# One decode block on one core: the third load of wo moved ahead of two loads of values, and 128 rows of w2 loaded by GpSimd to 32 partitions

## The chip, the core and the metric

The kernel runs on one NeuronCore of a Trainium2 chip. The core has five engines with instruction streams of their own: TensorE (PE, with its weight loads as PEld), VectorE (DVE), ScalarE (ACT), GpSimd (POOL) and SyncE (SP), and sixteen DMA engines that move data between HBM and the on-chip memory (SBUF, 128 partitions). The metric is the device time of one execution in microseconds (us); lower is better.

## What is computed

One token goes through an attention block and a second block, and the results are added. Cut to what matters:

```python
xn = layernorm(x)                                   # x: 1024 values
# A: 32 query heads, 4 key/value heads, 65536 positions of 128
q = xn @ wq                                         # wq 1024 x 4096
p = softmax(q . k_cache / sqrt(128));  o = p . v_cache
A = o @ wo                                          # wo 4096 x 1024
# B
h  = gelu(layernorm(xn) @ w1)                       # w1 1024 x 1024
hs = shift(h) @ w2                                  # shifts along a sequence of length 1
x1 = xn + hs                                        # w2 1024 x 1024
B  = x1 + gelu(layernorm(x1) @ w3) @ w4             # w3 1024 x 3584, w4 3584 x 1024
out = x + A + B
```

All inputs are bf16. With a sequence of one token every shift pushes its value out, so the vector that meets w2 is zero; the kernel loads w2 all the same and multiplies it by a zero vector (`g_bf`). The weights and the two caches together are 162 MiB, and each byte is read once.

## The kernel before, in words

**Slots and loads.** SBUF holds eight slots of 16 KB per partition (`slots_sb`). A load of a 4 MB piece of keys or values fills two slots (32 KB to each of the 128 partitions); a load of wo, w1 or w2 fills one (2 MB, 16 KB to each partition). All these loads are issued by SP, in one fixed order, on one DMA queue (q1 in the profile): `load` (line 315), `load2` (line 321) and, for the last pieces of w4, `load_pieces` (line 328). Before each issue SP waits (line 54) until the last user of the slot is done. So one load that waits for its slot holds back every load behind it in SP's order, even one whose own slot has long been free.

**The order.** `loads` (line 625) begins with wq in two loads, w1, w2 and w3 in two. Then `order` (line 632) alternates keys and values, values lagging five tiles behind, and ends by hand with the last values and the four loads of wo; w4 follows in three groups (line 639), the last one in pieces of two, one and one row per partition. `where` (line 301) gives each load its slots: values alternate between slots 4-5 and 0-1, so value tile 14 waits for the use of tile 12, and tile 15 for that of tile 13; wo 0 to 3 go to slots 2, 3, 6 and 7, the last two of which held the last keys; w4 goes to 4-5, 0 and 1.

**A head.** DVE turns each half tile of keys by a transpose (line 542) into the buffer `X`, PE forms the scores (line 555), ACT takes the exponentials (line 580), PE and ACT transpose them (lines 589, 592), and PE adds up the values (line 603). `combine` (line 610) gives the head's output, which `use_wo` (line 531) multiplies with its part of wo. The buffer `X` has two halves: half 0 is first used by the first transpose of keys, half 1 also by the small products.

**The small products.** `rows_mv` (line 454) issues the matmuls of a weight: for each row index of a partition and each quarter of the columns one matmul of 256 columns (line 460), so 32 for a weight of 1024 x 1024. A weight of 1024 rows stands as eight rows of 2 KB in each of 128 partitions. `use_w2` (line 509) adds the product to `xn`, normalizes the sum, and gives `xn3_bf` for w3.

**The beginning.** POOL sets constants until 8.15 us (lines 386 to 408) and has nothing to do later but one small power in each of three layer norms (line 446). ACT issues three small loads of x (lines 411 and 417) on a queue of its own (q10). DVE waits for them (line 420), and the first layer norm follows.

**The end.** PE multiplies the pieces of w4 as they land, DVE adds the result to the rest (`fin`, line 716), and SP and ACT issue the store (line 719).

Of the kernel before, what the change touches and what calls it, by code (L numbers as in the profile page):

```python
# [6 lines left out]
BF = mybir.dt.bfloat16  # L7
# [82 lines left out]
def _deps(q, reads, writes):  # L90
    for b in reads:
        for s, v in b.w.items():
            q.wait((s, v))
    for b in writes:
        for s, v in b.w.items():
            q.wait((s, v))
        for s, v in b.r.items():
            q.wait((s, v))


def _done(ev, reads, writes, partial=False):
    for b in reads:
        b.add_read(ev)
    for b in writes:
        if partial:
            b.add_write(ev)
        else:
            b.set_write(ev)


def _op(q, fn, reads=(), writes=(), partial=False):
    _deps(q, reads, writes)
    ev = q.op(fn, True)
    _done(ev, reads, writes, partial)
    return ev


def _grp(q, fns, reads=(), writes=(), partial=False):
    _deps(q, reads, writes)
    ev = None  # L120
    for i, fn in enumerate(fns):
        ev = q.op(fn, i == len(fns) - 1)
    _done(ev, reads, writes, partial)
    return ev
# [23 lines left out]
def _dma(q, chan, fn, reads=(), writes=(), partial=False):  # L148
    _deps(q, reads, writes)
    chan.n += 1  # L150
    ev = q.dma(fn, chan.sem, 16 * chan.n)
    _done(ev, reads, writes, partial)
    return ev
# [10 lines left out]
def bass_parallel_sum__gqa_block_cached__mixer_s_mlp__decode_kernel(  # L164
# [14 lines left out]
    P = 128  # L179
    D = A_x.shape[2]  # L180
# [5 lines left out]
    R = D // P  # L186
# [10 lines left out]
    EPS = 1e-5  # L197
    NS = 8
    PAD = 31
    SLOT = 8192  # L200

    with ExitStack() as es:
# [3 lines left out]
        def sb(name, shape, dt):  # L206
            return E(nc.sbuf_tensor(name, shape, dt))

        def ps(name, shape, dt):
            return E(nc.psum_tensor(name, shape, dt))  # L210

        def sem(name):
            return E(nc.semaphore(name))
# [25 lines left out]
        Ycur = sb("Ycur", [P, 4, 4, G], BF)  # L239
        slots_sb = sb("slots_sb", [P, NS, SLOT], BF)  # L240
        X = sb("X", [P, 2, SLOT], BF)
        S_sb = sb("S_sb", [P, NCH, 512], F32)
# [11 lines left out]
        cb_o = sb("cb_o", [P, R], F32)  # L254
        oP_bf = sb("oP_bf", [P, HKV, PAD + R + PAD], BF)
        xr_bf = sb("xr_bf", [P, RW], BF)
        accr = sb("accr", [P, RW], F32)
        g_bf = sb("g_bf", [P, R + 32], BF)
# [3 lines left out]
        h1g_bf = sb("h1g_bf", [P, R], BF)  # L262
        gh_bf = sb("gh_bf", [P, PAD + NT + PAD], BF)
        fin = sb("fin", [P, RW], BF)

        S_all = ps("S_ps", [P, 4 * 512], F32)
        S_ps = [S_all[:, 512 * i:512 * (i + 1)] for i in range(4)]
# [6 lines left out]
        q_dve = _Q("dve", sem("c_dve"))  # L274
        q_act = _Q("act", sem("c_act"))
        q_pool = _Q("pool", sem("c_pool"))
        q_sp = _Q("sp", None)
        ch_x = _DmaChan(sem("d_x"))
        ch_out = _DmaChan(sem("d_out"))
        ch_v = [_DmaChan(sem("d_v0")), _DmaChan(sem("d_v1"))]  # L280
        t_x, t_s, t_r, t_p, t_t, t_o = [sem("t_" + c) for c in "xsrpto"]
# [3 lines left out]
        b_const = _B(); b_xb = _B(); b_x = _B(); b_xn = _B(); b_xn2 = _B(); b_x1 = _B(); b_xn3 = _B()  # L285
        b_ln = _B(); b_qT = _B(); b_Y = _B(); b_Yc = _B(); b_misc = _B(); b_ge = _B()
        b_X = [_B(), _B()]
# [10 lines left out]
        X32 = X[:].bitcast(F32)  # L298
# [11 lines left out]
        def take(i, n, uses):  # L310
            for k in range(n):
                assert taken[i + k] == 0
                taken[i + k] = uses

        def load(i, src, width=SLOT):
            take(i, 1, 1)
            view = slots_sb[:, i, 0:width]
            _dma(q_sp, slots[i].chan, lambda e, view=view, src=src: e.dma_start(out=view, in_=src), writes=[slots[i].buf])
            return [(view, [slots[i].buf], i)]

        def load2(i, src, half=SLOT, chan=None):
            take(i, 2, 1 if half == SLOT else 2)
            view = slots_sb[:, i:i + 2, :].rearrange("p s c -> p (s c)")[:, 0:2 * half]
            _dma(q_sp, chan or slots[i].chan, lambda e, view=view, src=src: e.dma_start(out=view, in_=src), writes=[slots[i].buf, slots[i + 1].buf])
            bufs = [[slots[i].buf], [slots[i + 1].buf]] if half == SLOT else [[slots[i].buf, slots[i + 1].buf]] * 2
            return [(view[:, k * half:(k + 1) * half], bufs[k], i + k) for k in range(2)]
# [16 lines left out]

        wq_v = A_wq.rearrange("(p r) n -> p (r n)", p=P)
        w1_v = B_w1.rearrange("(p r) n -> p (r n)", p=P)
        w2_v = B_w2.rearrange("(p r) n -> p (r n)", p=P)
        w3_v = B_w3.rearrange("(p r) n -> p (r n)", p=P)
        w4_v = B_w4.rearrange("(p r) n -> p (r n)", p=P)

# [30 lines left out]
            return load2(i, A_v_cache[0, h, a * n:(a + 1) * n, :].rearrange("(p c) d -> p (c d)", p=P), chan=ch_v[a % 2])  # L380


        evs = []
        for t_, val in ((selGT_bf, 1.0), (selTT, 1.0), (ident_bf, 0.0), (ones_f, 1.0), (neghalf, -0.5), (permWE, 1.0), (maskA, 1.0),
                        (sel16, 1.0), (dmask, 0.0), (g_bf, 0.0), (xn_bf, 0.0), (xn2_bf, 0.0), (xn3_bf, 0.0), (oP_bf, 0.0), (gh_bf, 0.0)):
# [22 lines left out]
                                                          compare_op=ALU.not_equal, fill=1.0, base=-16 * j, channel_multiplier=1))  # L408
        b_const.set_write(ev)

        _dma(q_act, ch_x, lambda e: e.dma_start(out=xP_bf[:, :], in_=A_x[0, 0, :].rearrange("(p r) -> p r", p=P)), writes=[b_xb])
        _op(q_dve, lambda e: e.memset(xr_bf[:], 0.0), writes=[b_xr])
        x4 = A_x[0, 0, :].rearrange("(j m) -> j m", j=4)
        _deps(q_act, [], [b_xr])
        for j in (0, 2):
            ch_x.n += 1
            q_act.dma(lambda e, j=j: e.dma_start(out=xr_bf[32 * j + PAD:32 * j + PAD + 2, :], in_=x4[j:j + 2, :]), ch_x.sem, 16 * ch_x.n)
        b_xr.set_write((ch_x.sem, 16 * ch_x.n))
# [35 lines left out]
        def rows_mv(nkk, parts, st_fn, b_st, b_slot, b_out, first, last, k0=0):  # L454
            fns = []
            for kk in range(k0, k0 + nkk):
                for out_fn, mv_fn in parts:
                    for j in range(4):
                        fns.append(lambda e, kk=kk, j=j, out_fn=out_fn, mv_fn=mv_fn, st=(first and kk == k0), sp=(last and kk == k0 + nkk - 1):
                                   e.matmul(out_fn(j), st_fn(kk, j), mv_fn(kk, j), start=st, stop=sp, tile_position=(0, 32 * j), skip_group_check=True))  # L460
            _grp(q_pe, fns, reads=b_slot + [b_st], writes=b_out, partial=not first)

        def to_p(src, c0, n, b_src):
            _op(q_dve, lambda e: e.transpose(out=X32[:, 1, c0:c0 + 32 * n], in_=src), reads=b_src, writes=[b_X[1]], partial=c0 > 0)  # L464
# [31 lines left out]
        def at_border(vec, kk, t):  # L496
            c = kk + PAD * (t % 2)
            return vec[:, c:c + 32]

        def d_parts(view, c0):  # L500
            return [(lambda t: M1_ps[32 * t:32 * t + 32, c0:c0 + RW], lambda kk, t: view[:, kk * D + t * RW:kk * D + (t + 1) * RW])]
# [6 lines left out]

        def use_w2(ld):
            view, b = ld[0:2]  # L510
            rows_mv(R, d_parts(view, 0), lambda kk, t: g_bf[:, kk:kk + 32], b_const, b, [b_M1], True, False)
            to_p(M1_ps[:, 0:RW].rearrange("p (c r) -> p r c", r=R), 0, R, [b_M1])
            _op(q_dve, lambda e: e.tensor_tensor(out=x1[:], in0=xn[:], in1=X32[:, 1, 0:32 * R:32], op=ALU.add), reads=[b_xn, b_X[1]], writes=[b_x1])
            layer_norm(x1, b_x1, None, xn3_bf, b_xn3, 4)

        def use_w3(j, ld):
# [4 lines left out]
            if j == 3:  # L521
                to_p(S_all[:, 1024:1024 + FW].rearrange("p (c s) -> p s c", s=NT), 0, NT, [b_S[2], b_S[3]])
                gelu(NT, gh_bf[:, PAD:PAD + NT], b_gh)

# [85 lines left out]
        def combine(h):  # L610
# [10 lines left out]
            _op(q_dve, lambda e: e.reduce_sum(cb_o[:, :], cb_m[:, :, :].rearrange("p x r -> p r x"), axis=AX.X), reads=[b_cb], writes=[b_cb])  # L621
            _op(q_act, lambda e: e.activation(oP_bf[:, h, PAD:PAD + R], cb_o[:, :], ACTF.Copy), reads=[b_cb, b_const], writes=[b_oP[h]])  # L622

# [4 lines left out]
        n_kv = 4 * HKV  # L628
        order = [("k", i) for i in range(LAG)]
        for i in range(LAG, n_kv):  # L630
            order += [("v", i - LAG), ("k", i)]
        order += [("v", n_kv - 5), ("v", n_kv - 4), ("wo", 0), ("v", n_kv - 3), ("wo", 1), ("v", n_kv - 2), ("v", n_kv - 1), ("wo", 2), ("wo", 3)]
        for kind, i in order:
            loads.append((kind,) + divmod(i, 4) if kind != "wo" else (kind, i))
            if kind != "wo":
# [7 lines left out]
        _op(q_dve, lambda e: e.tensor_scalar(out=accr[:], in0=xr_bf[:], scalar1=ln_s[:, 1:2], scalar2=ln_s[:, 4:5], op0=ALU.add, op1=ALU.mult),  # L643
            reads=[b_xr, b_ln], writes=[b_accr])
        _op(q_dve, lambda e: e.tensor_tensor(out=accr[:], in0=accr[:], in1=xr_bf[:], op=ALU.add), reads=[b_xr, b_accr], writes=[b_accr])
        loaders = {"wq": load_wq, "w1": lambda i: load(i, w1_v[:, 0:SLOT]), "w2": lambda i: load(i, w2_v), "w3": load_w3, "wo": load_wo, "w4": load_w4,
                   "k": load_k, "v": load_v}
        doubles = {"wq", "w3", "k", "v"}

# [35 lines left out]
        for it in uses:  # L685
# [16 lines left out]
            elif kind == "v":  # L702
                h, n = args
# [51 lines left out]
```

## Time and profile before

| | |
|---|---|
| median of 3 runs | 406.3 us (406.21 to 406.33) |
| the profiled execution: its time, its span | 405.76 us, 404.0 us |
| bytes read from HBM | 169.87 MB, 420 GB/s over the span |
| busy share of the span: DMA queue q1 on 16 engines | 98.3% |
| PE, PEld, DVE, ACT, POOL | 38%, 17%, 45%, 19%, 2% |
| last landing of w4, then matmul, addition, store | 401.5 us, the rest to 404.0 us |

The span runs from the first to the last instruction of the profiled execution; 1.76 us of the execution's own time lie outside it. The profile cuts the span into slices and gives for each the busy share of the engines and of the DMA engines; it lists groups of instructions with their mean duration and the idle time before them; it follows the chain of work that ended last back from the last instruction; and it can print the instructions of a stretch in order of time, or the busy time of several stretches side by side. The trace also holds a record of each DMA packet: when it began, how long it took, its bytes and its queue. It does not say which of the sixteen engines carried it.

### The profile page before, as it was taken

The numbers are of one execution on the slowest core, as the hardware profiler recorded it, in microseconds if no ns is written. First come the engines' busy times: TensorE is split into PE (matmuls) and PEld (weight loads), VectorE is DVE, ScalarE is ACT, GpSimd is POOL, SyncE is SP. The second block draws the span as 40 slices with busy tenths as digits, with TensorE's granted clock in tenths as the row PEclk, the third lists the DMA queues.
The fourth block names the chain that finished last, engine by engine and source line by source line (L and its number), as shares of the span: only waits on it lengthen the run. The fifth ranks groups of instructions, "written<-read, shape, count | busy, mean of one in ns | idle before, by whom it ended". The sixth has DMA issues, their size and how long they took to land. (4 is left out here: it accounts for less than half of the span.)

```text
span 404.0 us, 3803 instructions
## 1 busy us (share of the span) xinstructions
PE 154.8 (38%) x1615; PEld 67.8 (17%) x1615; DVE 183.8 (45%) x137; ACT 75.3 (19%) x71; POOL 7.8 (2%) x38
## 2 busy tenths in 40 slices
PE   0165323244257041344561513257215152603705
PEld 0023110011023010111320101123101012301403
DVE  0135019998747263746545364748180931000200
ACT  1000000111762010191310002813010157200000
POOL 6010000000000000000000000000000000000000
PEclk9995565555556756565575565555956555666777
DMA  8999999999999999999999999999999999899995
GB/s 357 422 415 420 458 419 420 455 417 419 443 435 415 441 441 415 435 448 415 422 454 422 419 454 425 419 444 431 419 438 441 415 425 454 334 415 436 441 414 219
DMA packets 6937, 170.00 MB, mean 421 GB/s; under 512 B 904, under 2 KB 912, under 8 KB 1296
## 3 DMA queue, kind: packets, MB, share of 16 engines
q1 hardware_dynamic: 6772, 169.87, 98.3%
q8 instruction: 6, 0.10, 0.1%
q10 hardware_dynamic: 156, 0.01, 0.0%
q14 instruction: 3, 0.02, 0.0%
HBM read 169.87 MB, written 0.00 MB: 420 GB/s over the span
## 5 line engine op out<-in xcount | busy, mean ns | idle before, releaser
L542 DVE STREAM_TRANSPOSE X<-slots_sb 128x4096 f32<-128x4096 f32 x32 | 141.2, 4428 | 84.3 <-DMA slots_sb<-in_A_k_cache_dram 84.3
L555 PE MATMUL S_ps<-X,Ycur 128*32 128x512 bf16 x512 | 57.8, 596 | 139.9 <-PEq L64 126.3
L603 PE MATMUL OT_ps<-slots_sb,pT_sb 128*32 128x512 bf16 x512 | 50.9, 568 | 22.9 <-PEq L64 22.6
L567 ACT ACTIVATE S_sb<-S_ps 128x1024 f32<-128x1024 f32 x16 | 16.4, 1026 | 181.4 <-DVE mcol L566 161.4
L555 PEld LDWEIGHTS S_ps<-X,Ycur 128*32 128x32 bf16 x512 | 16.8, 124 | 176.6 <-issue 160.9
L580 ACT ACTIVATE p_sb<-S_sb,brun 128x1024 bf16<-128x1024 f32 x16 | 40.5, 2580 | 2.5 <-DVE brun L578 2.2
L603 PEld LDWEIGHTS OT_ps<-slots_sb,pT_sb 128*32 128x32 bf16 x512 | 19.9, 132 | 48.6 <-issue 46.0
L611 DVE TENSOR_TENSOR O_m<-OT_ps,selT_f 128x512 f32<-128x512 f32 x4 | 2.8, 691 | 52.1 <-PE OT_ps L603 52.1
L589 PE MATMUL PT_ps<-ident_bf,p_sb 128*128 128x128 bf16 x128 | 16.2, 307 | 18.5 <-PEq L64 18.5
L566 DVE TENSOR_REDUCE mcol<-S_ps 128x1 f32<-128x1024 f32 x16 | 19.1, 1195 | 8.6 <-PE S_ps L555 8.6
L592 ACT ACTIVATE pT_sb<-PT_ps 128x1024 bf16<-128x1024 bf16 x16 | 16.4, 1024 | 34.3 <-PE PT_ps L589 34.3
L589 PEld LDWEIGHTS PT_ps<-ident_bf,p_sb 128*128 128x128 bf16 x128 | 12.4, 138 | 24.2 <-issue 24.2
L460 PE MATMUL S_ps<-slots_sb,xn_bf 128*32 128x512 bf16 (+1 forms) x128 | 12.3, 556 | 10.4 <-DMA slots_sb<-in_B_w_dram 9.0
L460 PE MATMUL M_ps<-slots_sb,gh_bf 128*32 128x256 bf16 x112 | 5.7, 357 | 12.0 <-DMA slots_sb<-in_B_w_dram 12.0
L471 ACT ACTIVATE ge_a<-ge_b 128x8 f32<-128x8 f32 (+1 forms) x2 | 0.4, 217 | 52.2 <-DVE ge_b L470 52.2
L716 DVE TENSOR_TENSOR fin<-accr,M_ps 128x256 bf16<-128x256 f32 x1 | 0.4, 421 | 21.2 <-PE M_ps L460 21.2
L464 DVE STREAM_TRANSPOSE X<-S_ps 128x512 f32<-128x512 f32 (+1 forms) x3 | 2.6, 850 | 14.1 <-PE S_ps L460 14.1
L420 DVE CAST xP<-xP_bf 128x8 f32<-128x8 bf16 x1 | 0.2, 172 | 16.7 <-DMA xr_bf<-in_A_x_dram 16.7
L460 PEld LDWEIGHTS S_ps<-slots_sb,xn_bf 128*32 128x32 bf16 x128 | 4.5, 134 | 16.6 <-DMA slots_sb<-in_B_w_dram 9.8
L622 ACT ACTIVATE oP_bf<-cb_o 128x8 bf16<-128x8 f32 x4 | 0.8, 210 | 33.1 <-DVE cb_o L621 33.1
L460 PEld LDWEIGHTS M_ps<-slots_sb,gh_bf 128*32 128x32 bf16 x112 | 3.5, 123 | 14.2 <-DMA slots_sb<-in_B_w_dram 13.5
L434 PE MATMUL M_ps<-ln_s,ones_f 128*128 128x1 f32 x6 | 1.5, 328 | 10.6 <-DVE ln_s L433 10.6
(88 smaller groups left out, 59.1 us busy)
## 6 DMA issues: line engine op xcount, KB each, us to landing
slots_sb<-in_A_k_cache_dram SPq DMA_DIRECT2D x16, 4096.0 KB, 27.0
slots_sb<-in_A_v_cache_dram SPq DMA_DIRECT2D x16, 4096.0 KB, 26.8
slots_sb<-in_A_wq_dram SPq DMA_DIRECT2D x2, 4096.0 KB, 16.9
slots_sb<-in_A_wo_dram SPq DMA_DIRECT2D x4, 2048.0 KB, 26.4
slots_sb<-in_B_w_dram SPq DMA_DIRECT2D x2, 3584.0 KB, 32.5
slots_sb<-in_B_w_dram SPq DMA_DIRECT2D x3, 2048.0 KB, 25.9
slots_sb<-in_B_w_dram SPq DMA_DIRECT2D x1, 4096.0 KB, 26.2
slots_sb<-in_B_w_dram SPq DMA_DIRECT2D x1, 512.0 KB, 23.0
```

Source lines behind the costliest of these rows:

```text
L434: _op(q_pe, lambda e: e.matmul(M0_ps[:, c0:c0 + 1], ones_f[:, :], ln_s[:, 0:1], start=True, stop=True), reads=[b_ln, b_const], writes=[b_M0])
L460: e.matmul(out_fn(j), st_fn(kk, j), mv_fn(kk, j), start=st, stop=sp, tile_position=(0, 32 * j), skip_group_check=True))
L464: _op(q_dve, lambda e: e.transpose(out=X32[:, 1, c0:c0 + 32 * n], in_=src), reads=b_src, writes=[b_X[1]], partial=c0 > 0)
L542: turn = lambda e: e.transpose(out=X32[:, m, :], in_=K32)
L555: fns.append(lambda e, we=we, c_mid=c_mid, mv=mv: e.matmul(S_ps[bank][32 * c_mid:32 * c_mid + 32, :], Ycur[:, we, :, :].rearrange("p a g - ...
L566: _op(q_dve, lambda e: e.reduce_max(mcol[:, x:x + 1], S2, axis=AX.X), reads=[b_S[2 * i], b_S[2 * i + 1]], writes=[b_mcol], partial=x > 0)
L567: _tell(q_act, lambda e: e.activation(S_sb[:, 2 * x:2 * x + 2, :].rearrange("p s c -> p (s c)"), S2, ACTF.Copy), t_s, reads=[b_S[2 * i], b ...
L580: fn = lambda e, x=x: e.activation(p_sb[:, :, :, :, x], S_sb[:, 2 * x:2 * x + 2, :].rearrange("p s (c i) -> p s c i", i=32), ACTF.Exp, bia ...
L589: _taking(q_pe, [(t_t, 1) if c8 else (t_p, 1)], [lambda e, i=i, c=8 * c8 + i: e.transpose(out=PT_ps[:, i * P:(i + 1) * P], in_=p_sb[:, c / ...
L592: _tell(q_act, lambda e, c8=c8: e.activation(pT_sb[:, :, 32 * c8:32 * c8 + 32, :].rearrange("p a x g -> p x a g"), PT_ps[:, :].rearrange(" ...
L603: fns.append(lambda e, cl=cl, q4=q4, x0=x0: e.matmul(OT_ps[32 * q4:32 * q4 + 32, :], pT_sb[:, a, x0:x0 + 4, :].rearrange("p x g -> p (x g) ...
L611: _op(q_dve, lambda e: e.tensor_tensor(out=O_m[:, :, :], in0=OT_ps[:, :].rearrange("p (t d) -> p t d", t=4), in1=selT_f[:, :].unsqueeze(2) ...
```

## The change

It has two parts. In SP's order the third load of wo moves from behind the last two loads of values to ahead of them. And w2 is cut: SP loads its first 896 rows as seven rows to each of the 128 partitions; the last 128 rows are loaded by POOL, in three DMAs, to 32 partitions of `X`, half 0: six rows to each of the partitions 92 to 99 (two engines), two rows to each of 4 to 19 (four engines), six rows to each of 60 to 67 (two engines). Three tiny DMAs of x, into a tensor that nobody reads, stand between them. DVE first sets six rows' width of `X`, half 0, to zero in all partitions, and `use_w2` multiplies those six rows as well, 24 matmuls; with seven rows from the slot that is 52 matmuls instead of 32. POOL's DMAs stand in its queue behind the constants and ahead of the layer norms.

```diff
+    W2B = 7
...
+        pad_sb = sb("pad_sb", [16, 6, 8], BF)
...
+        ch_w2 = _DmaChan(sem("d_w2"))
...
-        w2_v = B_w2.rearrange("(p r) n -> p (r n)", p=P)
+        w2_v = B_w2[0:W2B * P, :].rearrange("(p r) n -> p (r n)", p=P)
...
+        def load_w2_part(p0, k, n, row):
+            src = B_w2[row:row + 4 * k * n, :].rearrange("(b a r) n -> a b (r n)", a=k, b=4)
+            dst = X[p0:p0 + 4 * k, 0, 0:n * D]
+            ch_w2.n += 1
+            q_pool.dma(lambda e: e.dma_start(out=dst, in_=src), ch_w2.sem, 16 * ch_w2.n)
+            return row + 4 * k * n
+
+        def load_pad(k, at):
+            src = A_x[0, 0, 0:16 * k].rearrange("(a b c) -> a b c", a=k, b=2)[:, :, 0:4]
+            dst = pad_sb[0:k, at:at + 2, 0:4]
+            ch_w2.n += 1
+            q_pool.dma(lambda e: e.dma_start(out=dst, in_=src), ch_w2.sem, 16 * ch_w2.n)
+
+        def load_w2_parts():
+            _deps(q_pool, [], [b_X[0]])
+            load_pad(15, 0)
+            row = load_w2_part(92, 2, 6, W2B * P)
+            row = load_w2_part(4, 4, 2, row)
+            load_pad(2, 2)
+            row = load_w2_part(60, 2, 6, row)
+            load_pad(7, 4)
+            assert row == D
+            b_X[0].add_write((ch_w2.sem, 16 * ch_w2.n))
...
+        _op(q_dve, lambda e: e.memset(X32[:, 0, 0:3 * D], 0.0), writes=[b_X[0]])
+        load_w2_parts()
         _dma(q_act, ch_x, lambda e: e.dma_start(out=xP_bf[:, :], in_=A_x[0, 0, :].rearrange("(p r) -> p r", p=P)), writes=[b_xb])
         _op(q_dve, lambda e: e.memset(xr_bf[:], 0.0), writes=[b_xr])
...
-            rows_mv(R, d_parts(view, 0), lambda kk, t: g_bf[:, kk:kk + 32], b_const, b, [b_M1], True, False)
+            rows_mv(W2B, d_parts(view, 0), lambda kk, t: g_bf[:, kk:kk + 32], b_const, b, [b_M1], True, False)
+            rows_mv(6, d_parts(X[:, 0, :], 0), lambda kk, t: g_bf[:, kk:kk + 32], b_const, [b_X[0]], [b_M1], False, False)
...
-        order += [("v", n_kv - 5), ("v", n_kv - 4), ("wo", 0), ("v", n_kv - 3), ("wo", 1), ("v", n_kv - 2), ("v", n_kv - 1), ("wo", 2), ("wo", 3)]
+        order += [("v", n_kv - 5), ("v", n_kv - 4), ("wo", 0), ("v", n_kv - 3), ("wo", 1), ("wo", 2), ("v", n_kv - 2), ("v", n_kv - 1), ("wo", 3)]
...
-        loaders = {"wq": load_wq, "w1": lambda i: load(i, w1_v[:, 0:SLOT]), "w2": lambda i: load(i, w2_v), "w3": load_w3, "wo": load_wo, "w4": load_w4,
+        loaders = {"wq": load_wq, "w1": lambda i: load(i, w1_v[:, 0:SLOT]), "w2": lambda i: load(i, w2_v, W2B * D), "w3": load_w3, "wo": load_wo, "w4": load_w4,
```

## The prediction, as it went on record

> **What bounds the kernel now.** I read the page's table of DMA queues first, then the chain of work that ended last, then the busy time of stretches around the one weak slice of the DMA row, and the instructions there in order of time.
>
> ```profile
> q1 hardware_dynamic: 6772, 169.87, 98.3%
> ...
> DMA 6%; PE 1%; SPq 0%; DVE 0%; issue 0%
> ```
>
> The one queue of big loads keeps the sixteen DMA engines 98.3% busy, while the busiest compute engine, DVE, stands at 45%. The chain in order of time (start, duration, what) shows the end:
>
> ```profile
> 377.57 0.43 SPq L339
> 378.00 0.04 issue
> 378.05 23.44 DMA slots_sb<-in_B_w_dram
> 401.49 0.04 issue
> 401.53 0.32 PE M_ps L460 x4
> 401.85 0.02 issue
> 401.88 0.42 DVE fin L716
> ```
>
> The last pieces of w4 are issued 23 us before they land: at the end the stream of loads is the limit, and whatever brings its last landing forward brings the end forward, one for one. Where does the stream lose time? Stretches (start:end, length, busy PE, PEld, DVE, ACT, POOL with counts, clock, DMA share, GB/s):
>
> ```profile
> 340.00:350.00 10.00, 5.19 (x48) 3.27 (x52) 0.00 (x0) 3.97 (x4) 0.00 (x0) 0.50 0.96 413
> 350.00:354.00 4.00, 2.81 (x48) 1.19 (x40) 0.00 (x0) 0.00 (x0) 0.00 (x0) 0.93 0.61 197
> 354.00:364.00 10.00, 0.27 (x4) 0.17 (x8) 0.00 (x0) 0.00 (x0) 0.00 (x0) 0.67 1.06 459
> ...
> 399.00:400.00 1.00, 1.00 (x32) 0.74 (x32) 0.00 (x0) 0.00 (x0) 0.00 (x0) 1.00 0.42 150
> 400.00:401.00 1.00, 0.55 (x16) 0.23 (x12) 0.00 (x0) 0.00 (x0) 0.00 (x0) 1.00 0.13 43
> ```
>
> There are two losses: a hole at 350 to 354, and a last stretch in which few engines still move. The hole is SP's wait:
>
> ```profile
> 332.42 0.43 SPq L318 DMA_DIRECT2D slots_sb<-in_A_wo_dram  x1
> ...
> 347.81 0.17 PEld L603 LDWEIGHTS OT_ps<-slots_sb,pT_sb 128*32 128x32 bf16 x8 [1.59 <-issue]
> ...
> 351.18 2.08 SPq L324 DMA_DIRECT2D slots_sb<-in_A_v_cache_dram  x2
> 353.30 0.94 SPq L318 DMA_DIRECT2D slots_sb<-in_A_wo_dram  x2
> ```
>
> After wo's second load (332.42) SP issues nothing until PE, which begins on value tile 12 at 347.8, has freed its slots (351.18). Meanwhile the queue runs dry. The two loads of wo behind the wait need no such slot.
>
> **The hole, engine by engine.** I strung the packet records into sixteen chains: a packet begins within some 5 ns of the end of the one before on its engine. A 32 KB packet takes 1.213 us on every chain, a 16 KB one 0.61. At the hole ten chains fall idle between 350.1 and 350.75, two at 351.3 and 351.5, four between 351.8 and 352.0; all start again between 352.1 and 352.9. Mean idle: 1.44 us. The first packet afterwards takes 1.48 to 2.26 us, 0.61 more than usual in the mean, so the hole costs an engine 2.05 us. Why are some later? Six code fetches of 16 KB (queue 8: at 35.0, 69.4, 84.1, 108.5, 384.7, 398.5) each hit one chain: 1.02 us for the fetch and 0.5 for the slower next packet (1.71 to 1.88), 1.5 together. Four come before the hole, two after it, by the chains on other engines. At the end fourteen chains finish between 399.2 and 400.4, the two with the late fetches at 400.97 and 401.02.
>
> **Moving wo's third load** adds no instruction. Its slot held the last keys, whose matmuls ended by 325.5, so SP can issue it right behind the second, near 332.9. It is 128 KB per engine, four packets' time, 4.86 us, and the chains then stay busy until 355.0 at the earliest, while the values, issued at 351.18, could start at 352.1. The hole closes whole. Per chain, from ends of before: an undisturbed one 399.25 - 2.35 idle - 0.45 slow packet = 396.45; one with an early fetch 399.25 - 0.3 - 0.75 = 398.2; one with a late fetch 401.0 - 2.35 - 0.45 = 398.2 (398.8 if it idled only 1.5). The last landing comes at 398.2 to 398.8, 2.2 to 2.8 us earlier. I take 2.6. A chain's own gain is not the gain of the whole: the ones that fall idle first win most and are not those that finish last.
>
> What is late next: values 14 and 15 now land behind wo's third load. Value 14 lands at 365, 15 near 375, against 363.2 and 372.9; its use takes 3.6 us, so w4's last pieces are issued some 2.5 us later than 375.5 to 378.5. The stream reached them 16 to 20 us after their issue; it now reaches them about 2.5 us sooner, so 11 us remain. Elsewhere the thinnest margin is value 13's issue, 3.15 us before the queue would be dry.
>
> **w2 in two parts, on the DMA engines.** Each of the sixteen loses one row of 2 KB in eight partitions, 16 KB, 0.61 us. From the code, three DMAs of 48, 32 and 48 rows on two, four and two engines give 24, 8 and 24 rows to each: 48 KB, 16 KB, 48 KB. Net: four engines +32 KB (+1.21 us), four at nothing, eight -0.61 us. The trace names no engine, so which chains these are it cannot say. If those with fetches are all relieved, the last landing is the later of 398.4 - 0.61 and 396.45 + 1.21: 0.6 us earlier still. If one of them carries the extra, it ends at 399.6: 1.2 us back. I take nothing, between the two, and keep -0.6 and +1.2.
>
> One price is unknown: a GpSimd packet between the big ones. The 16-byte packets of x took turns with 32 KB packets, and the next one took 1.213 to 1.23 us: nothing. The code fetch cost 0.4 over the 0.61 of its bytes and 0.5 behind it. So 0 to 0.9 for each of four packets (a partition's six rows lie together); I take 0, as for x, which is also a queue of several packets.
>
> [...]
>
> **The rest of w2's part lies beside other work.**
>
> ```profile
> 17.74 0.17 DVE L420 CAST xP<-xP_bf 128x8 f32<-128x8 bf16 x1 [16.69 <-DMA xr_bf<-in_A_x_dram]
> ...
> 20.52 0.56 POOL L446 TENSOR_TENSOR ln_s<-ln_s,neghalf 128x1 f32<-128x1 f32 x1 [12.37 <-DVE ln_s L444]
> ...
> 33.89 1.90 PE L460 MATMUL M_ps<-slots_sb,g_bf 128*32 128x256 bf16 x32 [0.65 <-DVE X L464]
> ...
> 42.45 2.86 PE L460 MATMUL S_ps<-slots_sb,xn_bf 128*32 128x512 bf16 x28 [3.62 <-DMA slots_sb<-in_B_w_dram]
> ```
>
> - DVE's memset of 3072 f32: between 0.17 us (its own 128x128 memset) and 3.3 (the 4096-wide transpose takes 4.43). I take 3.3. DVE idles 16.69 us there. ACT's two loads of x wait for the next memset, but their packets come at 13.6, behind the first load of x on that queue, so an issue near 4.7 instead of 1.25 costs nothing.
> - POOL's six issues: DMA issues on ACT and SP take 0.24 to 0.74 us, POOL's own longest stretch, eight selects, 2.6. I take 0.74: 4.4 us, against 12.37 idle ahead of the power. At 2.6 each (15.6) the first layer norm comes 3.3 us late, and SP's next load, w3's second, is issued at 25.4 with 14.5 us in hand: still nothing.
> - PE: 20 more matmuls at 1.90 / 32 = 0.059 us: 1.2 us, inside the 3.62 in which it waits for w3.
> - The new wait of w2's matmuls for POOL's DMAs holds PE, behind it the w3 matmuls, and through slot 5 SP's second load of keys. Four packets that each let a big one pass need 6.7 us: landed by 31, before 33.85. SP issues those keys at 35.9, 22 us before the queue would be dry, so the parts may land as late as 55.
>
> Sum: -2.6 us on the profiled 405.76 gives 403.2. The median of the runs is 406.3, 0.54 above it, so I predict 403.7.
>
> **Rivals.**
> 1. *The extra rows fall on an engine with a fetch.* For it: six of sixteen chains are late by 1.5 us, four carry more. Against: nothing names them. Last landing 399.6; gain 1.4: 404.9. Chance 0.22.
> 2. *The GpSimd packets cost as a code fetch does*, 0.9 each. Place: the engines with extra rows. An undisturbed one ends at 396.45 + 1.21 + 3.6 = 401.3, no gain: 406.6. Against: the packets of x. Chance 0.06.
> 3. *Slower: the parts land too late.* If POOL's DMAs cut the rows into small packets, each waits for a 32 KB packet. From a start near 13, a landing after 55 takes over 33 packets per engine (1.29 us each); from there PE's wait delays the keys and the stream one for one. At 512 bytes, 96 packets, the landing is near 130: some 75 us, 481. A start delayed on POOL by 25 us or more does the same. Chance 0.06. The first two rivals together (399.6 + 3.6 = 403.2) also end slower, 408.5; chance 0.03.
> 4. *The change does not do what it says*: the stall returns at w4's slots, or the hole is closed by nothing because SP waits for slot 6. Then 406.3. Against: the release at 325.5. Chance 0.05.
>
> **Chances and range.** The forecast, with the relieved case down to 403.0, holds 0.58. Faster by over 0.2% (under 405.5; about what a measurement can tell) holds that and rival 1: 0.80. Within 0.2%: rival 4, half of rival 2 and some of rival 1's tail, 0.09. Slower: the rest, 0.11. The range 402.7 to 405.6 takes in w2's bounds on either side of the forecast and leaves out rivals 2 and 3.
>
> **What the profile after would show.** wo's third load issued near 333 and no stretch under 0.9 DMA share at 350 to 354; values issued near 351 as before; w2's parts landed before 34; a last landing near 398.9 or earlier; ends of the chains closer than 1.8 us if the extra rows lie well. I am wrong if PE waits at w2 beyond 40, if the last landing is that of an engine with extra rows, or if a new hole opens behind 365.

## The result, and the profile after

| | before | after |
|---|---|---|
| median (18 runs each) | 406.13 us (405.82 to 406.56) | 405.38 us (404.84 to 405.80) |
| ratio, 95% interval | | 0.998 (0.9973 to 0.9987) |
| the profiled execution: time, span | 405.76 us, 404.0 us | 405.46 us, 403.5 us |

The kernel became 0.75 us faster, where 2.6 had been forecast. The time is inside the range, but most of the forecast gain is missing, so the question is where it went. The queue table (packets, MB, share of sixteen engines) and the shares of the chain of waits, on the page after:

```profile
q1 hardware_dynamic: 6772, 169.61, 98.3%
q0 software_dynamic: 336, 0.26, 0.2%
...
DMA 4%; PE 1%; SPq 0%; DVE 0%; issue 0%
```

0.26 MB have moved from q1 to GpSimd's queue q0, and the stream of loads still bounds the kernel. Its busy stretches (start:end, length, busy PE, PEld, DVE, ACT, POOL with counts, clock, DMA share, GB/s):

```profile
340.00:350.00 10.00, 4.32 (x36) 3.27 (x40) 0.00 (x0) 4.67 (x7) 0.00 (x0) 0.50 0.97 416
350.00:354.00 4.00, 4.00 (x44) 1.70 (x40) 0.00 (x0) 0.00 (x0) 0.00 (x0) 0.50 1.00 426
354.00:364.00 10.00, 2.10 (x28) 0.77 (x20) 0.00 (x0) 0.00 (x0) 0.00 (x0) 0.67 1.04 439
...
399.00:400.00 1.00, 0.81 (x24) 0.20 (x12) 0.00 (x0) 0.00 (x0) 0.00 (x0) 0.84 0.16 61
400.00:401.00 1.00, 0.64 (x12) 0.23 (x8) 0.00 (x0) 0.00 (x0) 0.00 (x0) 0.50 0.03 12
```

The hole at 350 to 354 is gone: the DMA share there went from 0.61 to 1.00. But the last stretch is thin: at 399 the share is 0.16 and at 400 it is 0.03, on average two or three engines of sixteen and then less than one, while the others are done. The chain of waits in order of time (start, duration, what) ends with them:

```profile
382.85 0.43 SPq L342
383.28 0.04 issue
383.33 17.49 DMA slots_sb<-in_B_w_dram
400.82 0.04 issue
400.86 0.43 PE M_ps L490 x4
401.29 0.02 issue
401.31 0.42 DVE fin L747
```

The last landing came 0.67 us earlier than before (400.82 against 401.49), where 2.6 had been worked out. SP's instructions around the hole (start, duration, engine, line, what):

```profile
334.28 0.90 SPq L321 DMA_DIRECT2D slots_sb<-in_A_wo_dram  x2
353.42 3.12 SPq L327 DMA_DIRECT2D slots_sb<-in_A_v_cache_dram  x2
356.58 0.44 SPq L321 DMA_DIRECT2D slots_sb<-in_A_wo_dram  x1
```

Two loads of wo now stand together at 334.3, as the order says. The values behind them were expected "near 351 as before" and are issued at 353.42: PE reached the end of value tile 12 some two microseconds later than before. Something earlier than the hole had made the loads late.

**How far apart the sixteen engines are.** Every big load leaves sixteen landings, one of each engine, and the packet records show them. The *spread* of a load is the time from its first landing to its last. PE waits for the last of them (in the chain above the last landing is at 400.82 and the matmul at 400.86), so spread at the end is time lost. Before, it was 1.75 us at 88 us and 1.87 at 331. After, it is 3.77 at both. It does not grow on the way: it jumps from 0.54 to 4.19 us between the two loads of wq, of which the second lands at 21.94 to 26.12, and GpSimd's 12 KB packets begin between 15.96 and 30.41 us. So what was lost came with the parts of w2, in the first 31 us, and the engines hardly even out again: the sixteen landings of the last piece of w4 still lie 3.09 us apart.

### The profile page after: what moved, and what is told of

It is laid out like the page before. It is cut to its first block, busy times and chain, and to the rows that moved or that the text cites. A ratio compares the mean times of both kernels' runs of the same rounds, so it can differ in the third digit from the quotient of the medians.

```text
span 403.5 us, 3851 instructions
## 1 busy us (share of the span) xinstructions
PE 159.5 (40%) x1635; PEld 70.1 (17%) x1635; DVE 186.5 (46%) x138; ACT 75.3 (19%) x71; POOL 11.4 (3%) x44
## 5 line engine op out<-in xcount | busy, mean ns | idle before, releaser
L634 PE MATMUL OT_ps<-slots_sb,pT_sb 128*32 128x512 bf16 x512 | 52.2, 582 | 25.0 <-PEq L64 24.7
L490 PE MATMUL S_ps<-slots_sb,xn_bf 128*32 128x512 bf16 (+1 forms) x128 | 13.8, 603 | 10.3 <-DMA slots_sb<-in_B_w_dram 8.0
L490 PE MATMUL M_ps<-slots_sb,oP_bf 128*32 128x256 bf16 x128 | 5.3, 346 | 0.2 <-issue 0.2
```

The costliest lines, as they stand in the source:

```text
L634: fns.append(lambda e, cl=cl, q4=q4, x0=x0: e.matmul(OT_ps[32 * q4:32 * q4 + 32, :], pT_sb[:, a, x0:x0 + 4, :].rearrange("p x g -> p (x g) ...
```

## The experiments

**The theories.** *P, the place:* a row costs time not only on the engine that carries it, but also on the engine that serves the partitions where it lands (the one that writes them in the big loads), when that is another one. *E, the rival:* a GpSimd packet costs its carrying engine more than its bytes do, wherever it lands. A third came with the third and fourth runs: *X*, that writes to another engine's partitions also slow all sixteen engines for a while, against *R*, that this belongs to the region of partitions 20 to 27. The trace names no engine, so which partitions are an engine's own and which are foreign to it is an assumption of the author's throughout, and no run shows it. All kernels but the eighth only change the order, the places or the number of w2's DMAs. Each time is compared with runs of the kernel before on the same chip (406.13 to 406.28).

The table holds the result of each, and from the packet records the spread of a load landing near 331 us, the *lag* (how much less the big loads and GpSimd's DMAs had moved by 330 us than in the kernel before, turned into microseconds of one engine, mean of sixteen) and the landings of the last piece of w4, as its semaphore counts them (some 0.45 us after the end of the packets).

| kernel | median, us | spread at 331 | lag at 330 | last piece lands, first to last engine |
|---|---|---|---|---|
| before | 406.13 | 1.87 | 0 | 399.64 to 401.49 |
| after | 405.38 | 3.77 | 0.57 | 397.73 to 400.82 |
| 1: order alone | 403.36 | 1.87 | -0.03 | 397.07 to 398.98 |
| 2: w2 alone | 408.17 | 3.43 | 0.51 | 401.67 to 403.46 |
| 3: part at 20 | 405.04 | 1.92 | 1.72 | 398.73 to 400.39 |
| 4: part at 64 | 407.67 | 5.74 | 0.85 | 399.53 to 403.08 |
| 5: one DMA | 403.64 | 1.94 | -0.08 | 397.25 to 399.00 |
| 6: part at 100 | 405.01 | 1.91 | 1.62 | 398.39 to 400.33 |
| 7: own places | 403.6 to 404.05, and 405.03 to 405.51 | 2.48 | 0.14 | 396.84 to 399.20 |
| 8: tiny DMAs only | 404.19 | 1.84 | 0.28 | 397.44 to 399.38 |

### 1 and 2: each half of the change by itself

The first kernel is the one before with the new order, the second is the changed kernel with the old order:

```diff
-        order += [("v", n_kv - 5), ("v", n_kv - 4), ("wo", 0), ("v", n_kv - 3), ("wo", 1), ("v", n_kv - 2), ("v", n_kv - 1), ("wo", 2), ("wo", 3)]
+        order += [("v", n_kv - 5), ("v", n_kv - 4), ("wo", 0), ("v", n_kv - 3), ("wo", 1), ("wo", 2), ("v", n_kv - 2), ("v", n_kv - 1), ("wo", 3)]
```

> Only wo's third load is moved; w2 is loaded as before. Theory P (the moved load is worth what was worked out, and the rows of w2 lost it again): the hole closes, the last landing comes 2.2 to 2.8 us earlier, 403.3 to 403.9 against a median of 406.1. Rival F (filling the hole is worth little, because the engines that finish last idled least in it): 405.3 to 405.9, about what both parts together gave.

Measured: 403.36 us (403.26 to 403.40), ratio 0.9928 (0.9915 to 0.9942). Its stretches, columns as above:

```profile
16.00:26.00 10.00, 5.13 (x44) 2.77 (x48) 3.06 (x15) 0.00 (x0) 0.56 (x1) 1.00 1.00 429
350.00:354.00 4.00, 3.47 (x48) 1.41 (x40) 0.00 (x0) 0.00 (x0) 0.00 (x0) 0.76 1.01 430
```

The hole is closed and the whole of its price comes back: 2.77 us, where the prediction had 2.6 for it. SP's row of the values shows that here they are issued near 351 as expected, and the chain of waits that the last landing comes 2.51 us earlier than before (401.49):

```profile
351.53 2.38 SPq L324 DMA_DIRECT2D slots_sb<-in_A_v_cache_dram  x2
...
381.39 17.59 DMA slots_sb<-in_B_w_dram
398.98 0.04 issue
```

> Only w2 is cut; SP's order is that of before. Theory P: two engines are 3.1 us late from 30 us on (twice 1.84 for 48 KB, less 0.61), the values they carry land late, PE frees tile 12's slots some 2 us later (353.4 instead of 351.2, as in the changed kernel), and the hole, still there, ends that much later: 407.3 to 408.3. Rival F (w2's part costs nothing or helps, and it is the load of wo that gives less): 405.5 to 406.3.

Measured: 408.17 us (408.03 to 408.58), ratio 1.0049 (1.0035 to 1.0063). The parts of w2 cost 408.17 - 406.13 = 2.04 us without the new order and 405.38 - 403.36 = 2.02 us with it, so the halves add up and the loss is w2's alone. The hole in this kernel, and SP's row behind it:

```profile
350.00:354.00 4.00, 4.00 (x44) 1.79 (x40) 0.00 (x0) 0.00 (x0) 0.00 (x0) 0.50 0.30 127
...
353.27 2.54 SPq L327 DMA_DIRECT2D slots_sb<-in_A_v_cache_dram  x2
```

The DMA share is 0.30 where it was 0.61: PE begins to multiply value tile 12 at 349.58 instead of 347.84, SP issues the values at 353.27 instead of 351.18, and the hole became longer.

### 3, 4 and 6: the same rows, bytes and packets, at other partitions

Only the first partition of one part changes. The packets, their number and order, and the bytes stay the same, and with them, as far as the code tells, the carrying engines (the trace names none), so E expects no difference. In the third kernel the first part goes to 20 to 27, in the sixth to 100 to 107, and in the fourth the third part goes to 64 to 71:

```diff
-            row = load_w2_part(92, 2, 6, W2B * P)
+            row = load_w2_part(20, 2, 6, W2B * P)
...
+            row = load_w2_part(100, 2, 6, W2B * P)
...
-            row = load_w2_part(60, 2, 6, row)
+            row = load_w2_part(64, 2, 6, row)
```

P forecast a spread of 1.9 us and 403.5 to 404.5 us with the part at 20, and a spread of 5.5 us and 406.4 to 407.4 us with the part at 64, both from the author's assumption of which engines' places these are.

> The changed kernel, the first part of w2's rows written to partitions 20 to 27 instead of 92 to 99; engines, bytes and packets as in the changed kernel. [...] Rival E (each packet of GpSimd's costs the engine that carries it, wherever it goes): spread 3.8 us and 405.4 as before.

> The changed kernel, the third part of w2's rows written to partitions 64 to 71 instead of 60 to 67; engines, bytes and packets as in the changed kernel. [...] Rival E: 405.4, spread 3.8 us.

Measured: 405.04 us (404.66 to 405.24; ratio 0.9972, 0.9961 to 0.9983) with the part at 20, and 407.67 us (407.33 to 408.04; ratio 1.0035, 1.0022 to 1.0049) with the third part at 64. The first lies above P's range, the second 0.27 us above it. At 64, the last landing moved to 403.08:

```profile
385.59 17.49 DMA slots_sb<-in_B_w_dram
403.08 0.04 issue
403.13 0.32 PE M_ps L490 x4
```

E falls: with the same packets, and as far as the code tells on the same engines, the spread at 88 us is 1.91 us with the part at 20, 3.77 in the changed kernel and 5.75 with the part at 64. The last step, 1.98 us, is about the time of four packets of 12 KB (0.46 us each, 1.84). The place decides the spread, and the sizes are near P's: at 331 us it is 1.92 where P had 1.9, and 5.74 where P had 5.5.

But P is not all. With the part at 20 the spread is as small as before, and P's range was 403.5 to 404.5 us, but the time hardly fell. What kept it up is lag: by 330 us all engines together are 1.72 us late. The stretch in which the parts land shows it in GB/s, in the third kernel:

```profile
16.00:26.00 10.00, 4.50 (x36) 2.25 (x36) 3.07 (x15) 0.00 (x0) 0.57 (x1) 1.00 0.99 359
```

against 429 in the first. The DMA share is 0.99 here and 1.00 there: the engines are busy all the time and move a sixth less. So busy engines were not engines at their pace here; the bytes beside the share tell the two apart.

> [...] Theory P: spread 1.9 us. Whether all engines slow down as they did at 20 to 27 (1.7 us in the mean by 330 us) is open: if any foreign place does that (X), 404.7 to 405.2; if it was the region of 20 to 27 (R), the mean loss is the changed kernel's 0.6 us and the time 403.7 to 404.2.

Measured: 405.01 us (404.74 to 405.10), ratio 0.9969 (0.9958 to 0.9980), spread 1.91 and lag 1.62 us: the same as with the part at 20. So it is not the region of 20 to 27, and R falls.

```profile
16.00:26.00 10.00, 4.46 (x36) 2.27 (x36) 3.07 (x15) 0.00 (x0) 0.57 (x1) 1.00 0.99 359
```

The sixteen landings of w2's seven rows, around 34 us, show where P itself comes short. With the part at 20 eight engines land between 33.50 and 33.78, four between 33.97 and 34.11, and four between 35.10 and 35.42; with it at 100 twelve land by 34.05 and four between 35.16 and 35.35. These are the eight, four and four engines of the prediction's count of bytes. P, as its author applied it, has no engine hit twice here, so two engines should stand late for the 48 rows that they receive, beside the four that carry 24 rows each: six in all. Four do. In these two kernels the place costs every engine about the same: between 15.5 and 27.5 us fourteen chains lost 1.28 to 1.51 us and two 1.73 to 1.83, so a receiving engine, whichever it is, paid at most some 0.4 us more than the rest, and not 1.84.

### 5: the same 128 rows, one to each partition, by one GpSimd DMA

```diff
-            load_pad(15, 0)
-            row = load_w2_part(92, 2, 6, W2B * P)
...
+            ch_w2.n += 1
+            q_pool.dma(lambda e: e.dma_start(out=X[:, 0, 0:D], in_=B_w2[W2B * P:, :]), ch_w2.sem, 16 * ch_w2.n)
...
-            rows_mv(6, d_parts(X[:, 0, :], 0), lambda kk, t: g_bf[:, kk:kk + 32], b_const, [b_X[0]], [b_M1], False, False)
+            rows_mv(1, d_parts(X[:, 0, :], 0), lambda kk, t: g_bf[:, kk:kk + 32], b_const, [b_X[0]], [b_M1], False, False)
```

The small DMAs and the memset go as well, since every partition gets its row; wo's third load stays moved, and w2 takes 32 matmuls. X expects no loss here if every engine writes these rows where it writes in the big loads, which is the author's assumption.

> [...] Theory X (what the changed kernel loses beyond the two late engines comes from rows written into partitions that another engine serves): no loss, 403.2 to 403.6, like the order alone (403.36). Rival G (any GpSimd DMA among the big loads takes some 0.6 us from all engines): 403.8 to 404.2.

Measured: 403.64 us (403.60 to 403.69), ratio 0.9936 (0.9922 to 0.9949). Spread and lag are those of the first kernel, 1.94 and -0.08 us, and so are the GB/s:

```profile
16.00:26.00 10.00, 5.07 (x52) 2.70 (x52) 3.06 (x15) 0.00 (x0) 0.57 (x1) 1.00 1.00 430
```

The time is 0.04 us above X's range and below G's. The last landing is at 399.00 against 398.98 in the first kernel, and the span is the same, 401.6 us; the 0.28 us between the two times lie outside the span (2.01 us in the mean, against 1.77). So the same bytes over the same GpSimd queue cost nothing in the stream when each engine writes an equal share (four packets of 4 KB). It was not GpSimd's queue as such, nor the bytes.

### 7: the same cut, with the rows in "own places"

```diff
-            load_pad(15, 0)
-            row = load_w2_part(92, 2, 6, W2B * P)
-            row = load_w2_part(4, 4, 2, row)
-            load_pad(2, 2)
+            load_pad(14, 0)
+            row = load_w2_part(88, 2, 6, W2B * P)
+            row = load_w2_part(0, 4, 2, row)
+            load_pad(3, 2)
```

The parts go to partitions 88 to 95, 0 to 15 and 60 to 67. The author chose them and the tiny DMAs so that each row would be written by the engine that writes its partitions in the big loads; that this is so no run shows, and "own places" is only a name for the choice.

> [...] Theory P with X: spread 1.9 us, no mean loss; the last landing is that of the four engines with extra rows, 1.2 us above the undisturbed, or of a fetch: 403.0 to 404.0. Rival E (the packets themselves cost their engine): spread 3.8 us and 405.2 to 405.6.

Ten runs fell into two groups: 403.60, 403.65, 403.75 and 404.05 us, and six of 405.03 to 405.51; the median is 405.06, ratio 0.9963 (0.9951 to 0.9975). The profiled execution belongs to the lower group (403.65). In it the lag is 0.14 us, and the 32 KB packets that began between 15.5 and 27.5 us show what happens beside the parts more plainly than any total. Each row is one chain, five packets in order, in nanoseconds:

```
own places     1213 1213 1213 1213 1213 (all sixteen chains, but one packet of 1220)
part at 20     1389 1646 1313 1518 1642
               1442 1348 1678 1693 1733
               1376 1582 1278 1608 1642 (all sixteen chains: 1.3 to 1.8 us too long in all)
after          1213 1213 1221 1304 1214 (most chains: 0.1 to 0.25 too long in all)
               1546 1625 1407 1701 1549 (one chain: 1.76 too long in all)
```

In the changed kernel two other chains lost 1.14 and 1.16 us: the loss there is that of three chains, not of all sixteen. With the rows in own places no 32 KB packet is slowed in this stretch (1.213 us, one 1.220); the packets of 12 KB take their 0.46 us, and the spread is 2.48 us, where P with X had said 1.9 and the balance of bytes alone gives 1.84.

Two more profiled executions of the same kernel were to tell why six runs were longer:

> The kernel with the rows in their own places once more, for one look: its ten runs fell into two groups, 403.6 to 404.05 and 405.0 to 405.5, and the profile was of the first. If this look is of the second group: theory L (a code fetch near the end falls on an engine with extra rows) expects clean packets of 1.21 us at 16 to 23 us, no mean loss, and one chain some 1.5 us after the others at the end; rival C (the DMAs of GpSimd start from another engine in some runs, so that rows go to foreign places) expects packets of 1.3 to 1.6 us at 16 to 23 us and a mean loss of 0.5 us or more.

> The same kernel and the same question, for a second look in case the first is of the lower group: L, clean packets at 16 to 23 us and one late chain at the end; C, packets of 1.3 to 1.6 us there and a mean loss.

They took 403.94 and 403.92 us, both of the lower group, so neither reading of the upper group could be decided. Its spans are 403.1 to 403.6 us against 401.6 to 402.1 in the lower one, so its loss lies inside the span, and its times are near what E had given. The cause stays open: every profile of this kernel is of the lower group, and what is said here of its packets and spread is shown for that group alone.

### 8: the new order and three tiny DMAs

This kernel is the first one with three small GpSimd DMAs of x, of 15, 10 and 7 partitions, into the tensor that nobody reads; w2 is loaded whole by SP.

```diff
+        load_pad(15, 0)
+        load_pad(10, 2)
+        load_pad(7, 4)
```

> The order alone, w2 loaded as before, and three tiny GpSimd DMAs of x (15, 10 and 7 engines) that nobody reads. Theory X: 403.3 to 403.6, like the order alone. Rival G (the GpSimd queue's small packets and completions cost the stream): 403.7 to 404.2.

Measured: 404.19 us (404.00 to 404.39), ratio 0.9950 (0.9936 to 0.9963), 0.83 us above the first kernel (0.68 if each is taken against the runs of before on its own chip), with a lag of 0.28 us. Some 0.3 us of it lie outside the span (2.08 us against 1.77). Its 96 tiny packets carry next to no bytes (the page gives q0 0.00 MB), and still some 32 KB packets between 13.5 and 20 us took 1.25 to 1.53 us. So it is not only the bytes that slow the others. The time is in G's range and outside X's. But G's price on any GpSimd DMA did not show in the fifth kernel, and X could be kept only if the tiny writes count as foreign, while in the seventh kernel three tiny DMAs to the same tensor leave only 3 of the 90 packets of 32 KB that began between 13.5 and 20 us above 1.225 us (here 16 of 85). What the tiny DMAs cost is measured; why is open.

## Why the prediction was wrong, step by step

**What bounds the kernel: right.** The stream bounds it before and after, and its last landing sets the end.

**The hole: right.** It was priced at 2.2 to 2.8 us, 2.6 taken; the order alone gains 406.13 - 403.36 = 2.77. In that kernel the last packet of w4 ends at 398.55 (401.03 before), inside the predicted 398.2 to 398.8, and two code fetches come after the hole as before. Two figures on the way were off without harm to the sum: 401.0 - 1.5 - 0.45 is 399.05 and not 398.8, and fourteen chains finished by 399.9, not 400.4 (by the signals of the last piece, 399.64 to 400.34, less 0.45).

**The step that failed: w2 in two parts.** "I take nothing, between the two, and keep -0.6 and +1.2": the part measured +2.0, beyond the worse of the two ends. The bytes per carrying engine were right, and so was "I take 0" for a surcharge of the packets: most 12 KB packets took 0.46 us, their share of 1.213 us for 32 KB, and in the seventh kernel's profile no 32 KB packet beside them was slowed. What the working lacked is the other end of the transfer: it priced a row by the engine that carries it, and never by the partitions that it is written to. The runs show two losses from that:

- *Spread.* In the changed kernel two engines stood some 3.6 us behind the relieved ones at 35 us, where the balance of bytes gave 1.84 (1.23 + 0.61). The part at 64 added 1.98 us to the spread; the parts at 20 and 100 took some 1.9 away, with the same packets. P would account for an engine that carries 24 rows and receives 24 more; why two engines and not one stood so far back in the changed kernel is not shown.
- *Lag.* Beside the parts other packets took longer, and the place decided how much. With the parts at 20 or 100 all sixteen chains lost 1.3 to 1.8 us between 15.5 and 27.5 us, and the lag by 330 us is 1.6 to 1.7 us; in the changed kernel three chains lost 1.1 to 1.8 and the others 0.1 to 0.25, and the lag is 0.57; in the seventh kernel it is 0.14.

From the first kernel to the changed one the last landing moved by 1.84 us (398.98 to 400.82), and it was late by that much all the way: from 40 us to 395 us the last engine of each load lands 1.9 to 2.0 us later than in the first kernel. The mean of the sixteen landings is 0.6 us later up to 336 us and 0.9 from 366 on (around 355 the values are issued 1.9 us later than in the first kernel and the engines that are ahead fall idle); the last engine is 1.85 us behind the mean at the end instead of 0.90. The rest of the 2.02 us, some 0.2, lies outside the span: 1.94 us in the mean of the changed kernel's runs against 1.77.

P and X need to know which engine writes which partitions, and that is the author's assumption, not shown by a run. The spreads of the third and fourth kernels (1.92 and 5.74 us, where P had 1.9 and 5.5) and the clean packets of the seventh (1.213 us) fit it; the number of late engines in the third and sixth (four, where P has six) does not.

**What the balance could give: 0.9 us at most.** In the first kernel the sixteen landings of the last piece lie between 397.07 and 398.98 with a mean of 398.08, so a perfect balance is worth 0.9 us, a little more than the 0.6 that the prediction saw in it. No form of the cut came below the order alone: 403.64 in one DMA, 403.6 at best in own places, against 403.36. The order alone is the fastest version that was run.

**Values "issued near 351 as before": wrong in the changed kernel (353.42), right in the first (351.53).** It is the late engines again, which reach SP by way of PE's use of tile 12 (it begins at 349.73 instead of 347.84). With it fell what the prediction had said of the chains if the extra rows lie well: their ends, expected closer than 1.8 us, were 3.09 us apart.

**The costs beside other work: right.** In the changed kernel (start, duration, engine, line, what, idle time before it and what ended it):

```profile
1.51 2.62 DVE L439 MEMSET X<- 128x3072 f32 x1 [1.51 <-PEq L771]
...
8.60 0.78 POOL L397 DMA_DIRECT2D pad_sb<-in_A_x_dram  x1 [0.41 <-issue]
...
20.95 0.57 POOL L476 TENSOR_TENSOR ln_s<-ln_s,neghalf 128x1 f32<-128x1 f32 x1 [8.73 <-DVE ln_s L474]
...
38.12 0.83 PE L490 MATMUL M_ps<-X,g_bf 128*32 128x256 bf16 x24
...
44.39 3.18 PE L490 MATMUL S_ps<-slots_sb,xn_bf 128*32 128x512 bf16 x32 [2.62 <-DMA slots_sb<-in_B_w_dram]
```

The memset took 2.62 us (3.3 estimated), POOL's issues 0.56 to 0.78 us each (0.74), the power ran 0.43 us later than before, and the 24 matmuls on `X` 0.83 us, after which PE still waited 2.62 us for w3. None of them holds anything up.

**The rivals.** The measured 405.38 lies near the first rival's 404.9, but not by its mechanism: the spread is there at 26 us, before the first code fetch (37.9). The second rival is excluded by the packets of the seventh kernel, the third by the parts, whose last 12 KB packet began at 30.41 us, the fourth by the first kernel.

**What stays open.** Which engine writes which partitions; why the part at 92 to 99 costs three chains much and the others little (0.57 us in the mean), and the parts at 20 and at 100 all sixteen the same, three times as much in the mean; how rows that a few engines carry slow the packets of all the others; what the tiny DMAs of the eighth kernel do; and the two groups of the seventh kernel.

## What to carry to other kernels

A transfer has two ends: when rows are shifted from one DMA engine to another to even out their loads, do not count only what each engine carries: here the same packets written to other partitions moved the time by up to 2.6 us (405.04 against 407.67). Where every engine wrote an equal share (the fifth kernel, four packets of 4 KB each), the stream lost nothing: the last landing came at 399.00 against 398.98. See from the landings of one load how far apart the engines are. Before such a balance is worked at, look at what it can give at most (the last end less the mean of the ends, here 0.9 us). And where a stream is the bound, read the GB/s beside the DMA share: the engines moved 359 GB/s at a share of 0.99 in one kernel and 429 at 1.00 in another.

## What the runs showed of the hardware beyond what was expected

- With GpSimd's rows at partitions 20 to 27 or 100 to 107, 32 KB packets on all sixteen engines took mostly 1.3 to 1.7 us instead of 1.213 for some ten microseconds; with the same packets at 92 to 99 thirteen of sixteen chains lost 0.1 to 0.25 us in five packets.
- A GpSimd DMA of 128 rows of 2 KB to 128 partitions, in the middle of a full stream, slowed no packet: each of its sixteen engines carried four packets of 4 KB, and the 32 KB packets beside them took 1.213 us.
- Three DMAs of a few hundred bytes were worth 0.83 us of a kernel's time (404.19 against 403.36).
- The time outside the span was 1.74 to 1.77 us in the mean in the kernels without GpSimd DMAs and 1.91 to 2.08 in those with them (those run five times or more): 0.1 to 0.3 us that no view of the span shows.
- In the changed kernel a spread between the sixteen engines that arose by 26 us was 3.77 us at 88 us and still 3.77 at 331.
